# Attention with two MLPs: the mask's threshold computed on GpSimd in place of ScalarE

## The chip, the cores and the metric

The kernel runs on one core of a Trainium2 chip. A core has five engines with instruction queues of their own that are worked off in order: TensorE (PE; its weight loads are shown apart as PEld), VectorE (DVE), ScalarE (ACT), GpSimd (POOL) and SyncE (SP, which here only issues transfers). An instruction waits at the head of its queue until what it needs has been done on other engines, and everything behind it on that engine waits with it. The metric is the device time of one execution in microseconds (us).

## The reference

Attention over 4 batches, 8 heads, 576 positions and 64 features per head. A score counts only if it lies within tau of its row's maximum; the softmax is over what is left. The result goes through a gated MLP (512 to 1536 to 512) and a squared-ReLU MLP (512 to 2048 to 512).

```python
scores = scale * np.matmul(q, k.transpose(0, 1, 3, 2))
thresh = np.max(scores, axis=-1, keepdims=True) - tau
scores = np.where(scores >= thresh, scores, -1000000000.0)
scores = scores - np.max(scores, axis=-1, keepdims=True)
attn = np.exp(scores)
attn = attn / (np.sum(attn, axis=-1, keepdims=True) + 1e-09)
return np.matmul(attn, v).astype(np.float32)
...
x = _moe_ref(x=x, **moe_kwargs)      # silu(x @ w_gate) * (x @ w_val) @ w_out
return _moe2_ref(x=x, **moe2_kwargs) # relu(x @ w_in) ** 2 @ w_out
```

## The kernel before

There are two stages. The first, up to about 455 us, is attention in 144 tiles of 128 query rows by 576 keys (nine tiles for a pair of heads, 16 pairs). The second is the MLPs. While attention runs, matmuls of the gated MLP for batches that are done are put between its own on PE (`fill_group`, names `xs_m`, `m_th`, `m_u`, `w`), and weights are loaded and split into two parts of lower precision (`Loader`, names `wr`, `wf`, `w`).

Tile t goes through these steps, each a function of its own:

- `QK(t)`, L575, PE: scores into one of only two score buffers `s`, so QK(t+2) can't start before MASK(t) has read its buffer.
- `RED(t)`, L587, DVE: `nm`, the negative row maximum.
- `EXP(t)`, L593, ACT: exp(score - maximum) into `e`; and `thr` = maximum - tau, 128x1, one number per row, which is the instruction that changes (L595, or L598).
- `MASK(t)`, L604, DVE: sets e to zero where the score is under `thr`, and sums the row.
- `RCP(t)`, L610, DVE: `r`, the reciprocal of the sum. `NORM(t)`, L615, POOL: e times r.
- `TR(t)`, L635, PE, two tiles later: transposes of e. `PH` and `PL` (L655, L658, L665, L673, L56) take them out of PSUM in two parts `pt`, and `AV`, L694 (L691 for the first batch) multiplies by the values `vs`.

POOL has other work in its one queue: the low part of half of the weights (`w`, L56, which waits for a copy on ACT), the low part of k (`raw`, L56), the values' two parts (`vs`, L52 and L56), a small copy for the tail of each head (`qt`, L52), the low part of some `pt` (L56, from `tf`) and of the MLP's `m_u`. On ACT, `thr` stands beside exponentials and PSUM copies.

The program is written tile after tile, but a list scheduler then sets each engine's order by its own estimates of when each instruction can start, with the offsets in `early0` and `early` as priorities. So an edit of one instruction's engine changes the order of others as well, on every engine. The names below, such as `thr_5118`, carry a running number; `thr_240` is the threshold of tile 4 (tiles count from 0), `thr_267` of tile 5, `thr_1785` of tile 48, `thr_3094` of tile 75 and `thr_5118` of tile 120.

Of the kernel before, what the change touches and what calls it, by code (L numbers as in the profile page):

```python
# [18 lines left out]
P = 128  # L19
# [937 lines left out]
def pack(inputs):  # L957
# [48 lines left out]
    "u1": ("P", "P"),  # L1006
    "u2": ("A", "D"),
    "qs": "A",
    "thr": "A",
    "wl": "PD",  # L1010
    "live": (3, 2),
    "fill": 6,
# [35 lines left out]
```

## Time and profile before

| what | value |
|---|---|
| median of 3 runs (lowest, highest) | 1199.45 us (1198.36, 1200.13) |
| the profiled execution's own time | 1198.72 us |
| its span, first to last instruction | 1196.9 us |
| PE busy in the span | 1162.6 us (97%) |
| DVE, ACT, POOL busy | 868.2 (73%), 652.1 (54%), 293.8 us (25%) |
| L595, the threshold on ACT | 144 instructions, 42.3 us |
| first and last start of L595 | 12.3 and 451.8 us |

The busy shares are of the whole span. POOL does nothing after attention, so its 25% stands for a far fuller queue within the first 455 us. A busy PE is not PE at its peak, but time in which PE is not busy is lost for sure, since its work is the longest of all. "PEclk" is the granted clock of TensorE as a share of full speed.

### The profile page before, as it was taken

The numbers are of one execution on the slowest core, as the hardware profiler recorded it, in microseconds if no ns is written. First come the engines' busy times: TensorE is split into PE (matmuls) and PEld (weight loads), VectorE is DVE, ScalarE is ACT, GpSimd is POOL, SyncE is SP. The second block draws the span as 40 slices with busy tenths as digits, with TensorE's granted clock in tenths as the row PEclk, the third lists the DMA queues.
The fourth block names the chain that finished last, engine by engine and source line by source line (L and its number), as shares of the span: only waits on it lengthen the run. The fifth ranks groups of instructions, "written<-read, shape, count | busy, mean of one in ns | idle before, by whom it ended". The sixth has DMA issues, their size and how long they took to land.

```text
span 1196.9 us, 20191 instructions
## 1 busy us (share of the span) xinstructions
PE 1162.6 (97%) x7008; PEld 1074.8 (90%) x7008; DVE 868.2 (73%) x2143; ACT 652.1 (54%) x1622; POOL 293.8 (25%) x417
## 2 busy tenths in 40 slices
PE   5999998999999999999999999999999999999998
PEld 4555887999999999999999999999999899999997
DVE  6877997799989895789965954468449748754443
ACT  5777887888777774545432532145546425533221
POOL 4445875676776663000000000000000000000000
PEclk9999998999999999999999999999999999999999
DMA  5664452444334310332310300003002201100111
GB/s 177 151 182 127 127 134 66 109 116 110 94 97 106 93 36 1 108 104 80 98 36 7 108 29 1 1 18 104 21 1 80 62 1 54 36 1 1 53 54 53
DMA packets 40853, 84.79 MB, mean 71 GB/s; under 512 B 5936, under 2 KB 6960, under 8 KB 40752
## 3 DMA queue, kind: packets, MB, share of 16 engines
q1 hardware_dynamic: 40752, 83.52, 24.9%
q8 instruction: 55, 0.90, 0.3%
q14 instruction: 46, 0.38, 0.1%
HBM read 52.23 MB, written 4.72 MB: 48 GB/s over the span
## 4 chain that ended last, share of the span: by engine, by line
PE 79%; DVE 9%; DMA 3%; ACT 3%; issue 2%; POOL 2%; SPq 1%; POOLq 0%; DVEq 0%; ACTq 0%
PE mm L219 30%; PE mm L310 15%; PE mm L264 9%; PE s L575 5%; PE bank L635 5%; PE bank L219 4%; PE bank L264 4%; PE bank L694 4%; PE bank L691 3%; DMA wr<-in_w_dram 2%; DVE e L604 2%; DVE nm L587 1%; POOL e L615 1%; DMA raw<-in_qkv_dram 1%; DVE xs_k L56 1%
## 5 line engine op out<-in xcount | busy, mean ns | idle before, releaser
L219 PE MATMUL mm<-xs_k,w 128*128 128x384 f32 (+1 forms) x2400 | 413.2, 330 | 0.5 <-ACT x L48 0.5
L219 PEld LDWEIGHTS mm<-xs_k,w 128*128 128x128 f32 x2400 | 407.8, 188 | 2.5 <-ACT x L48 0.7
L310 PE MATMUL mm<-w,k_u 128*128 128x512 f32 x864 | 201.3, 391 | 0.3 <-DVE k_u L56 0.3
L310 PEld LDWEIGHTS mm<-w,k_u 128*128 128x128 f32 x864 | 161.5, 188 | 34.0 <-DVE k_u L56 1.0
L635 PE MATMUL bank<-ident,e 128*128 128x128 f32 x720 | 162.9, 278 | 6.4 <-POOL e L615 1.9
L219 PE MATMUL bank<-xs_m,w 128*128 128x288 f32 x720 | 137.1, 325 | 2.4 <-DVE xs_m L56 1.7
L615 POOL TENSOR_SCALAR e<-e,r 128x576 f32<-128x576 f32 x144 | 113.8, 791 | 83.6 <-DVE r L610 34.4
L604 DVE SCALAR_TENSOR_TENSOR e<-s,thr,e 128x577 f32<-128x577 f32 x144 | 117.0, 813 | 14.7 <-ACT thr L595 7.2
L48 ACT ACTIVATE k_u<-k_th 128x384 fp32r<-128x384 f32 (+1 forms) x148 | 76.3, 516 | 90.0 <-DVE k_th L294 47.0
L587 DVE TENSOR_REDUCE nm<-s 128x1 f32<-128x576 f32 x144 | 108.3, 753 | 17.7 <-PE s L575 16.6
L635 PEld LDWEIGHTS bank<-ident,e 128*128 128x128 f32 x720 | 95.2, 141 | 28.7 <-issue 15.9
L56 DVE TENSOR_TENSOR k_u<-k_th,k_u 128x384 fp32r<-128x384 f32 (+1 forms) x148 | 81.2, 549 | 47.8 <-ACT k_u L48 47.4
L219 PEld LDWEIGHTS bank<-xs_m,w 128*128 128x128 f32 x720 | 111.1, 189 | 5.1 <-DVE xs_m L56 3.4
L593 ACT ACTIVATE e<-s,nm 128x576 f32<-128x576 f32 x144 | 107.4, 746 | 14.3 <-PE bank L635 7.0
L655 ACT ACTIVATE pt<-bank 128x384 fp32r<-128x384 f32 (+1 forms) x216 | 92.1, 437 | 35.1 <-PE bank L635 28.9
L293 ACT ACTIVATE k_th<-mm 128x384 f32<-128x384 f32 x96 | 46.3, 483 | 111.0 <-PE mm L219 110.9
L264 PE MATMUL mm<-k_u,w 128*128 128x384 f32 (+1 forms) x624 | 106.1, 327 | 0.6 <-DVE k_u L56 0.4
L264 PEld LDWEIGHTS mm<-k_u,w 128*128 128x128 f32 x624 | 103.7, 188 | 1.0 <-DVE k_u L56 0.6
L694 PE MATMUL bank<-pt,vs 128*128 128x256 f32 (+1 forms) x480 | 93.5, 324 | 1.3 <-POOL pt L56 1.2
L575 PE MATMUL s<-kh,qs 128*128 128x288 f32 x256 | 78.1, 319 | 14.2 <-DVE qs L484 7.2
L294 DVE TENSOR_TENSOR k_th<-k_th 128x384 f32<-128x384 f32 x96 | 53.3, 555 | 52.4 <-ACT k_th L293 52.1
L48 ACT ACTIVATE w<-wf 128x256 fp32r<-128x256 f32 x116 | 46.8, 413 | 57.0 <-DVE wf L140 43.3
(90 smaller groups left out, 1697.0 us busy)
## 6 DMA issues: line engine op xcount, KB each, us to landing
wr<-in_w_dram SPq DMA_DIRECT2D x106, 256.0 KB, 3.0
raw<-in_qkv_dram SPq DMA_DIRECT2D x15, 896.0 KB, 4.7
kh<-land SPq DMA_DIRECT2D x60, 144.0 KB, 2.5
kl<-raw SPq DMA_DIRECT2D x60, 144.0 KB, 2.7
xF<-in_w_dram SPq DMA_DIRECT2D x30, 256.0 KB, 2.9
out_dram<-xF SPq DMA_DIRECT2D x18, 256.0 KB, 2.0
qs<-land SPq DMA_DIRECT2D x30, 144.0 KB, 2.4
qs<-raw SPq DMA_DIRECT2D x30, 144.0 KB, 2.6
```

What stands on the lines that cost most here:

```text
L48: nc.scalar.activation(out, in_, AF.Copy)
L56: e.tensor_tensor(out, a, b, op=ALU.subtract)
L219: mm(pt[:, :n], w[:, a, col + c * P : col + (c + 1) * P], xs[:, b, c, :], start=(i == 0), stop=(i == len(TERMS) - 1),)
L264: mm(pt[:, :n], w[:, a, 2 * DM + m * P : 2 * DM + (m + 1) * P], u[:, b, :], start=(k == 0), stop=(k == last),)
L310: mm(pt, u[:, b, s * P : (s + 1) * P], w[:, a, DM : 2 * DM], start=(k == 0), stop=(k == last),)
L575: mm(sp[:, cols], l, r[:, cols], start=(n_ == 0), stop=(n_ == len(pairs) - 1),)
L587: nc.vector.tensor_reduce(nm, sv, axis=AX.X, op=ALU.max, negate=True)
L593: nc.scalar.activation(e[:, :S], st[t]["s"][:, :S], AF.Exp, bias=st[t]["nm"])
L604: nc.vector.scalar_tensor_tensor(e, st[t]["s"][:, : S + 1], st[t]["thr"], e, op0=ALU.is_ge, op1=ALU.mult, accum_out=sum_)
L615: nc.gpsimd.tensor_scalar(e, e, scalar1=r, scalar2=1.0, op0=ALU.mult, op1=ALU.mult)
L635: mm(dst[:, j], e[:, c0 : c0 + P], ident, is_transpose=True, start=(j == 0), stop=(j == len(cols) - 1),)
L694: mm(o[:, :n], hd["vs"][:, SLOT[k % 5], :], pt[:, k, lo : lo + n], start=(k == 0), stop=(k == 9))
```

## The change

One entry of the configuration table is changed. `EXP` then takes its other branch, and `thr` comes from a GpSimd instruction that works out nm times -1 plus (-tau) for 128x1 elements, at L598 in place of the ScalarE one at L595.

```diff
     "qs": "A",
-    "thr": "A",
+    "thr": "P",
     "wl": "PD",
```

The scheduler then orders all five queues anew. Three places are shown, `+` for rows that stand there now, `-` for rows that stood there before. First POOL's queue at the start, around the thresholds of tiles 4 and 5 (`raw` is the low part of k, `qt` a small copy that waits for a transfer, `w_0` a weight's low part that waits for ACT).

```order
+L598 TENSOR_SCALAR thr_214<-nm_213,tau_n 128x1
+L56 TENSOR_TENSOR raw_205<-raw_205,land_207 128x288 x2
 L615 TENSOR_SCALAR e_97<-e_97,r_209 128x576
 L615 TENSOR_SCALAR e_95<-e_95,r_235 128x576
-L56 TENSOR_TENSOR raw_205<-raw_205,land_207 128x288 x2
 L52 TENSOR_SCALAR qt_122<-qs_333 128x64
+L56 TENSOR_TENSOR w_0_143<-xF,w_0_143 128x256
+L598 TENSOR_SCALAR thr_240<-nm_239,tau_n 128x1
+L598 TENSOR_SCALAR thr_267<-nm_266,tau_n 128x1
 L615 TENSOR_SCALAR e_96<-e_96,r_262 128x576
-L56 TENSOR_TENSOR w_0_143<-xF,w_0_143 128x256
```

The thresholds of tiles 4 and 5 stand behind six pieces of other work, and the weight's low part has moved ahead of them.

Second POOL's queue around the threshold of tile 120 (`vs` are the two parts of the next head's values).

```order
 L52 TENSOR_SCALAR vs_5379<-raw_5109 128x5x64
 L56 TENSOR_TENSOR vs_5379<-raw_5109,vs_5379 128x5x64
+L598 TENSOR_SCALAR thr_5118<-nm_5117,tau_n 128x1
 L615 TENSOR_SCALAR e_97<-e_97,r_5113 128x576
+L598 TENSOR_SCALAR thr_5163<-nm_5162,tau_n 128x1
 L615 TENSOR_SCALAR e_95<-e_95,r_5158 128x576
```

Nothing else moved there; the threshold stands behind both `vs` instructions and ahead of the NORM of the tile before.

Third PE's queue ahead of QK of tile 77 (the four rows of L575), which waits for MASK of tile 75; L219 are matmuls of the MLP, L694 those with the values.

```order
-L694 MATMUL bank_84<-pt,vs_2964 128x256
+L219 MATMUL bank_85<-xs_m_3173,w_0_143 128x288 x3
+L635 MATMUL bank_83<-ident,e_96 128x128 x2
+L219 MATMUL bank_85<-xs_m_3173,w_0_143 128x288
+L694 MATMUL bank_84<-pt,vs_2964 128x256 x3
+L219 MATMUL bank_85<-xs_m_3173,w_0_143 128x288 x2
+L694 MATMUL bank_84<-pt,vs_2964 128x256 x2
+L219 MATMUL bank_85<-xs_m_3173,w_0_143 128x288 x3
 L575 MATMUL s_108<-kh_3006,qs_3005 128x288
 L575 MATMUL s_108<-kl_3007,qs_3005 128x288
 L575 MATMUL s_108<-kh_3006,qs_3005 128x288
 L575 MATMUL s_108<-kl_3007,qs_3005 128x288
```

Here 16 matmuls stand ahead of QK that were not in this place before, in place of one there and two transposes a little earlier: 13 more than before. At QK of tile 122, which waits for MASK of tile 120, the number of matmuls ahead is the same as before.

## Rows read from the trace of the kernel before

**Rows 1.** Stages: us from:to, length, busy of each engine (instructions), PEclk, DMA share, GB/s.
```profile
30.00:120.00 90.00, 85.79 (x443) 52.44 (x442) 71.45 (x178) 66.16 (x172) 41.99 (x59) 1.00 0.57 153
120.00:200.00 80.00, 70.56 (x476) 64.31 (x475) 76.25 (x185) 66.11 (x178) 57.55 (x76) 0.96 0.42 114
200.00:455.00 255.00, 252.43 (x1915) 246.05 (x1914) 226.70 (x556) 200.78 (x513) 172.66 (x242) 1.00 0.38 92
```

**Rows 2.** PE's waits from 30 to 480 us: us in total, times, longest.
```profile
PE s L575 <- DVE e L604: 2.9, 4, 1.5
PE bank L264 <- POOL w L56: 1.8, 2, 1.6
...
PE bank L635 <- ACT pt L673: 1.7, 3, 1.0
PE bank L635 <- POOL e L615: 1.6, 3, 0.9
PE bank L694 <- POOL pt L56: 1.2, 3, 0.8
PE bank L635 <- ACT x L48: 0.9, 2, 0.7
PE bank L264 <- ACT w L48: 0.8, 1, 0.8
```

**Rows 3.** Threshold and mask by line: busy us, mean ns | idle before, releasers.
```profile
L604 DVE SCALAR_TENSOR_TENSOR e<-s,thr,e 128x577 f32<-128x577 f32 x144 | 117.0, 813 | 14.7 <-ACT thr L595 7.2 <-ACT e L593 5.0 <-PE bank L691 1.1
...
L595 ACT ACTIVATE thr<-nm,tau_n 128x1 f32<-128x1 f32 x144 | 42.3, 295 | 12.4 <-DVE nm L587 9.9 <-DVE r L610 1.6
```

**Rows 4.** POOL's smallest instructions, by tile and by line: ns least/median/most.
```profile
L52 POOL TENSOR_SCALAR qt<-qs x32: 235/246/433, 7.2 to 428.9; 128x64 fp32r<-128x64 f32 x32
...
L397 POOL MEMSET e<- x3: 99/99/100, 0.7 to 0.8; 128x1 f32 x3
```

**Rows 5.** Timeline of tile 4 (start, us; in brackets the idle time before, and its end).
```profile
21.82 0.81 DVE L604 SCALAR_TENSOR_TENSOR e<-s,thr,e 128x577 f32<-128x577 f32 x1
...
22.04 0.24 POOL L52 TENSOR_SCALAR qt<-qs 128x64 fp32r<-128x64 f32 x1
...
22.89 0.16 DVE L610 RECIPROCAL r<-sum 128x1 f32<-128x1 f32 x1
...
23.24 0.75 POOL L615 TENSOR_SCALAR e<-e,r 128x576 f32<-128x576 f32 x1 [0.96 <-DVE r L610]
...
23.55 0.40 PE L575 MATMUL s<-kh,qs 128*128 128x288 f32 x1
...
23.96 0.73 POOL L56 TENSOR_TENSOR w<-xF,w 128x256 fp32r<-128x256 f32 x1
```

**Rows 6.** Timeline of tile 120.
```profile
383.85 0.74 ACT L593 ACTIVATE e<-s,nm 128x576 f32<-128x576 f32 x1
...
384.80 0.82 DVE L604 SCALAR_TENSOR_TENSOR e<-s,thr,e 128x577 f32<-128x577 f32 x1
...
385.66 0.87 POOL L56 TENSOR_TENSOR vs<-raw,vs 128x320 fp32r<-128x320 f32 x1
...
386.79 0.29 PE L575 MATMUL s<-kh,qs 128*128 128x288 f32 x1
```

**Rows 7.** Timeline of tile 75.
```profile
249.42 0.82 DVE L604 SCALAR_TENSOR_TENSOR e<-s,thr,e 128x577 f32<-128x577 f32 x1 [0.32 <-ACT thr L595]
...
250.00 0.88 POOL L56 TENSOR_TENSOR vs<-raw,vs 128x320 fp32r<-128x320 f32 x1
...
250.30 0.40 PE L575 MATMUL s<-kh,qs 128*128 128x288 f32 x1
```

**Rows 8.** Timelines of POOL and DVE at tile 48.
```profile
153.13 0.74 POOL L56 TENSOR_TENSOR w<-xF,w 128x256 fp32r<-128x256 f32 x1 [1.52 <-ACT w L48]
...
154.53 1.74 POOL L56 TENSOR_TENSOR raw<-raw,land 128x288 fp32r<-128x288 f32 x2
...
152.88 0.81 DVE L604 SCALAR_TENSOR_TENSOR e<-s,thr,e 128x577 f32<-128x577 f32 x1
```

## The prediction

> **What bounds the kernel now.** I read the busy time by stage first. From 200 to 455 us PE is busy 252.43 of 255 us, so it sets the end of attention there; from 120 to 200 us it is busy 70.56 of 80, with DVE at 76.25 as the fuller engine and a mean granted clock of 0.96; from 30 to 120 us PE lacks 4.2 us of 90 [rows 1]. All three together leave 16.2 us in which PE stands idle, and since the change touches no instruction after attention, a gain can come from little else. Whether it comes depends on who ends those waits. In the list of PE's waits the three kinds that ACT ends make 1.7 + 0.9 + 0.8 = 3.4 us in 6 waits, the three longest kinds that POOL ends 1.8 + 1.6 + 1.2 = 4.6 us in 8, and MASK ends 2.9 us in 4 [rows 2]. So ACT, which the change relieves, holds PE up for less time than POOL, which it loads.
>
> Then the threshold itself. MASK sat idle 7.2 us for `thr` and 5.0 us for the exponential [rows 3]. The first number looks like the gain, and the reader should see why it is not. ACT sends `thr` off right behind the exponential: at tile 120 the exponential ends at 383.85 + 0.74 = 384.59 and MASK starts at 384.80, with the threshold between [rows 6]. Without it MASK still waits for the exponential, and wins some 0.2 us. And in front of none of PE's four waits for MASK had that MASK started right behind its threshold: DVE was at other work until then. I book 0.2 us, one such MASK in the first 30 us, which the list leaves out.
>
> **What the change removes, adds and moves.** Removed: 144 ACT instructions of 295 ns, 42.3 us [rows 3]. ACT is not full in any stage, 66 of 80 us at its fullest [rows 1], so this is worth what PE's waits for ACT shrink by: one threshold of 0.295 us in front of each of the 6 waits gives 1.8 us, none gives 0, all of the waits gone gives 3.4. I take 1.8, since an average of one threshold stands between two such copies.
>
> Added: 144 POOL instructions of 128x1. The trace has none of them. From below, a memset of 128x1 takes 99 ns; from above, a TENSOR_SCALAR of 128x64, the same operation with 63 more columns, 246 ns in the median and 433 at most [rows 4]. A NORM of 576 columns takes 0.75 us, so 512 columns more than 64 cost 0.50, one column 1 ns; that leaves 0.19 us for one column, which I take. Hand-offs: NORM starts 23.24 where its reciprocal ended 23.05, 0.19 later [rows 5]; the way out to DVE has no row here, it lies between 0 and that, and I take 0.05, since the 0.21 us between exponential and MASK at tile 120 already hold most of a threshold of 0.295. A threshold on a free POOL then reaches MASK 0.43 us after RED's end, while the exponential, which waits for the same RED, takes 0.74 [rows 6]. So on a free queue the threshold is wholly hidden. The price is in the queue.
>
> That price has two parts. The smaller: POOL's own work that PE waits for gets later by the thresholds in front of it. 8 waits, 0.19 each, would be 1.5 us; not every run of POOL work that ends in such a wait has a threshold in it, so I take half, 0.8 (bounds 0 and 1.5).
>
> The larger: the head of POOL's queue. `thr` now waits until the instruction ahead of it is done, and MASK waits for `thr`, with DVE's whole queue behind it and QK two tiles later on PE. I went through the new POOL order, took for each threshold the end of the instruction ahead of it in the trace of before, added 0.19 + 0.05, and compared it with the start of its MASK; then subtracted the time by which QK of two tiles later started after that MASK's end. Two tiles show the working. Tile 120: `vs` ends 385.66 + 0.87 = 386.53, so MASK could start at 386.77 in place of 384.80, 2.0 late; its old end was 385.62 and QK came at 386.79, 1.1 us of slack, so 0.85 reaches PE [rows 6]. Its neighbours on POOL and on PE are as before, so nothing covers that. Tile 75: `vs` ends at 250.88, MASK would be 1.7 late, and QK started within 0.06 us of its end [rows 7], so all of 1.7 reaches PE by this account. But there the scheduler has put 13 more matmuls ahead of that QK; at the stage's rate of 255 us for 1915 matmuls, 0.13 each [rows 1], they fill 1.7 us. This one is covered.
>
> Over all tiles ten keep something past the slack, from tile 4 (2.2) to tile 120 (0.85), 10.9 us in sum. Then I take off what the order itself answers. Tiles 75 and 77, 2.1: covered by matmuls that moved. Tiles 4 and 5, 3.4: the account uses `w` at its old time of 23.96, but `w` has moved up; right behind `qt`, which ended 22.28, it would end 23.0, MASK start 23.25 in place of 21.82, 1.4 late against a slack of 0.9 [rows 5], so I keep 1.0 of the 3.4. Tile 48, 2.0: the low part of k ahead of its threshold ran after two `w` that took from 153.13 to 154.53, and these now stand behind it [rows 8]; MASK was at 152.88, so between 0.6 and 2.0 stays, and I keep 1.0. That leaves 10.9 - 2.1 - 2.4 - 1.0 = 5.4.
>
> A page of the Trainium skill speaks against this engine too: GPSIMD Engine Reference, section Key points, says that GpSimd shares its SBUF interfaces with VectorE and that they contend when a DVE instruction has two SBUF inputs. The 128x64 copy took between 235 and 433 ns [rows 4], which agrees with some such disturbance without showing its cause. By that rule every late threshold could cost 0.43 in place of 0.19, 2.4 us over ten tiles. I leave this out of the sum.
>
> **Sum.** 5.4 (late masks) + 0.8 (POOL's other work) - 1.8 (ACT) - 0.2 (the threshold's own wait) = +4.2 us. The profiled execution took 1198.72, 0.7 under the median of 1199.45; the same 4.2 on the median gives 1203.7.
>
> **Rivals.** First, faster: ACT's relief wins. Late masks cost nothing because the scheduler moved work under each as it did at tile 75, and all six waits for ACT go: -3.4 - 0.2 gives 1195.8. For it speaks that ACT's exponentials and copies share one queue; against it that tile 120 has no cover. It decides if fewer than about 1.2 us of late masks reach PE while the 3.4 us go whole, since then 2.4 us (0.2%, about what a measurement of this kernel tells from no change) are won.
>
> Second, no difference that can be told: masks are late, but half of the 5.4 is absorbed because a PE that waits once finds its next inputs ready. Then 2.7 + 0.8 - 1.8 - 0.2 = +1.5, 1201.0. For it speaks that the waits of DVE and of PE are counted here tile by tile, as though none made up for another; against it that PE from 200 us on is full and has nothing to make up with.
>
> Third, slower by more than 9 us: neither moved matmuls nor moved POOL work cover anything, and each threshold hits the waits in POOL's queue: 10.9 + 1.5 - 0 = +12.4, 1211.9. The stage from 120 to 200 us, where DVE is nearly full and the clock already sags, is where it would show. Against it stand the moves read at tiles 75, 4 and 48.
>
> That the change does nothing at all is excluded by the new order.
>
> **How the numbers follow.** The forecast case, slower by 2.4 to 9 us, gets 0.46; slower by more 0.07; no difference 0.26; faster 0.21. So faster 0.21, same 0.26, slower 0.53. The range: from 1196.5, which leaves the lower half of the faster case out, to 1209.5, under the third rival; about 1 in 10 is left on each side. The forecast case by itself reaches from 1201.9 to 1208.5.
>
> **What would show it.** In the profile after, L598 on POOL should show about 0.19 us each, 27 us in all, and L595 be gone from ACT. MASK (L604) should show idle time that POOL's `thr` ended, more than the 7.2 us of before, in waits of 1 to 2 us behind `vs`, `raw` and `w`; at tile 120 PE should wait for MASK some 0.8 us ahead of QK of tile 122. PE's busy time from 200 to 455 us should stay, and its idle time in the attention stage grow by 4 us. I am wrong if MASK waits less for POOL than it did for ACT, if a threshold takes 0.1 us or 0.4, or if the idle time from 120 to 200 us shrinks because the order there happens to fit better, which this account can't see.

## The result and the profile after

The changed kernel takes 1209.14 us in the median (1208.33 to 1210.54 in 6 runs), the kernel before 1199.05 beside it; the ratio of the means is 1.0081, with an interval of 1.0066 to 1.0095. That is 9.7 us slower (0.81% of 1199.45), with 1.7 to either side; the medians lie 10.1 apart. The forecast was slower by 4.2, 1203.7, in a range from 1196.5 to 1209.5. The sign and the range hold. The size does not: 9.7 is more than twice 4.2, and just outside the forecast case's own range, which ended at 1208.5.

The profiled execution took 1208.33 us, with a span of 1206.6. Busy time by engine, first on its page:

```profile
PE 1166.8 (97%) x7008; PEld 1076.0 (89%) x7008; DVE 867.9 (72%) x2143; ACT 628.1 (52%) x1478; POOL 333.4 (28%) x561
```

PE's busy time grew by 4.2 us from 1162.6, for the same 7008 matmuls, and its idle time in the span by 5.5, from 34.3 to 39.8. The profile models the ends of matmuls, so a short delay can also lie inside what it counts as busy. ACT lost 24.0 us of 652.1 and POOL's busy time grew by 39.6. The 144 instructions on ACT summed to 42.3 us [rows 3], but they overlapped the exponential ahead of them (at tile 120 it ends at 384.59, and MASK, which needs the threshold of 0.295 too, starts 0.21 later [rows 6]); so only 24.0 us of busy time went.

The same lines as in [rows 3], and the new one (busy us, mean ns, then idle time of the engine ahead of them and what ended it):

```profile
L598 POOL TENSOR_SCALAR thr<-nm,tau_n 128x1 f32<-128x1 f32 x144 | 44.8, 312 | 52.3 <-DVE nm L587 31.3 <-DVE r L610 18.6 <-PE s L575 2.1
...
L604 DVE SCALAR_TENSOR_TENSOR e<-s,thr,e 128x577 f32<-128x577 f32 x144 | 117.2, 815 | 29.3 <-ACT e L593 13.5 <-POOL thr L598 9.7 <-POOL e L615 1.6
```

MASK's idle time doubled, from 14.7 to 29.3 us. The threshold now ends 9.7 of it where it ended 7.2; but the exponential ends 13.5 where it ended 5.0. So the larger part of the growth isn't put down to the threshold, which is the first sign that MASK's new wait isn't the whole story.

The stages of [rows 1] (us from:to, length, busy time of PE, PEld, DVE, ACT, POOL, granted clock, DMA):

```profile
30.00:120.00 90.00, 84.62 (x429) 51.01 (x430) 67.80 (x173) 60.41 (x139) 49.19 (x89) 1.00 0.54 140
120.00:200.00 80.00, 70.47 (x471) 62.90 (x469) 76.79 (x185) 60.97 (x152) 65.89 (x97) 0.97 0.50 136
200.00:455.00 255.00, 248.96 (x1859) 240.26 (x1859) 222.23 (x543) 181.79 (x419) 188.97 (x318) 1.00 0.37 91
```

PE's idle time in them is 5.4 + 9.5 + 6.0 = 20.9 us, where it was 16.2. The growth of 4.7 is nearly all from 200 us on (3.5) and from 30 to 120 us (1.2). It is about half of the 9.7.

PE's waits of [rows 2], from 30 to 480 us (total, times, longest):

```profile
PE s L575 <- DVE e L604: 3.9, 10, 0.7
PE bank L665 <- ACT pt L655: 3.0, 3, 1.5
PE bank L635 <- POOL e L615: 2.9, 3, 1.6
PE bank L264 <- POOL w L56: 1.8, 3, 0.8
...
PE bank L635 <- ACT x L48: 1.0, 2, 0.5
...
PE bank L264 <- ACT w L48: 0.8, 2, 0.4
```

MASK ends ten of them where it ended four. And the three longest kinds that ACT ends make 4.8 us where they made 3.4: the engine that was relieved holds PE up for longer. The list of before has a fourth kind that ACT ends, which [rows 2] leaves out; with all kinds ACT's are 4.1 us before and 5.9 after.

```profile
PE bank L665 <- ACT pt L655: 0.7, 2, 0.4
```

Tile 120, in three stretches of the timeline after (start, us, engine; in brackets the idle time before it and what ended it):

```profile
394.99 0.87 POOL L56 TENSOR_TENSOR vs<-raw,vs 128x320 fp32r<-128x320 f32 x1
395.85 0.27 POOL L598 TENSOR_SCALAR thr<-nm,tau_n 128x1 f32<-128x1 f32 x1
...
396.15 0.82 DVE L604 SCALAR_TENSOR_TENSOR e<-s,thr,e 128x577 f32<-128x577 f32 x1 [1.07 <-POOL thr L598]
...
397.03 0.40 PE L575 MATMUL s<-kh,qs 128*128 128x288 f32 x1 [0.52 <-DVE e L604]
```

It went as forecast for this tile in kind: the threshold stands behind `vs`, MASK waits 1.07 us for it with DVE idle, and PE waits for MASK ahead of QK of tile 122, for 0.52 us where 0.85 had been worked out.

### The profile page after: what moved, and what is told of

Same layout as the page of the kernel before. It is cut to its first block, busy times and chain, and to the rows that moved or that the text cites. A ratio compares the mean times of both kernels' runs of the same rounds, so it can differ in the third digit from the quotient of the medians.

```text
span 1206.6 us, 20253 instructions
## 1 busy us (share of the span) xinstructions
PE 1166.8 (97%) x7008; PEld 1076.0 (89%) x7008; DVE 867.9 (72%) x2143; ACT 628.1 (52%) x1478; POOL 333.4 (28%) x561
## 4 chain that ended last, share of the span: by engine, by line
PE 82%; DVE 7%; POOL 6%; issue 3%; ACT 2%; DMA 0%; SPq 0%; POOLq 0%; ACTq 0%; DVEq 0%
PE mm L219 34%; PE mm L310 16%; PE mm L264 9%; PE bank L219 5%; PE s L575 4%; PE bank L635 4%; PE bank L694 3%; PE bank L264 3%; PE bank L691 3%; DVE e L604 2%; POOL e L615 1%; DVE nm L587 1%; POOL pt L56 1%; POOL raw L56 1%; DVE xs_m L56 1%
## 5 line engine op out<-in xcount | busy, mean ns | idle before, releaser
L219 PE MATMUL mm<-xs_k,w 128*128 128x384 f32 (+1 forms) x2400 | 413.2, 330 | 0.5 <-ACT x L48 0.5
L219 PEld LDWEIGHTS mm<-xs_k,w 128*128 128x128 f32 x2400 | 407.8, 188 | 2.5 <-ACT x L48 0.7
L635 PE MATMUL bank<-ident,e 128*128 128x128 f32 x720 | 162.1, 279 | 8.8 <-POOL e L615 4.9
L219 PE MATMUL bank<-xs_m,w 128*128 128x288 f32 x720 | 137.2, 325 | 2.4 <-DVE xs_m L56 1.3
L604 DVE SCALAR_TENSOR_TENSOR e<-s,thr,e 128x577 f32<-128x577 f32 x144 | 117.2, 815 | 29.3 <-ACT e L593 13.5
L635 PEld LDWEIGHTS bank<-ident,e 128*128 128x128 f32 x720 | 95.1, 142 | 30.1 <-issue 13.2
L615 POOL TENSOR_SCALAR e<-e,r 128x576 f32<-128x576 f32 x144 | 110.3, 766 | 31.2 <-DVE r L610 15.2
L219 PEld LDWEIGHTS bank<-xs_m,w 128*128 128x128 f32 x720 | 111.1, 189 | 6.1 <-DVE xs_m L56 2.5
L56 DVE TENSOR_TENSOR k_u<-k_th,k_u 128x384 fp32r<-128x384 f32 (+1 forms) x148 | 81.1, 549 | 46.2 <-ACT k_u L48 45.8
L575 PE MATMUL s<-kh,qs 128*128 128x288 f32 x256 | 78.8, 322 | 15.9 <-DVE e L604 7.6
L694 PE MATMUL bank<-pt,vs 128*128 128x256 f32 (+1 forms) x480 | 92.6, 323 | 1.4 <-DVE xF L706 0.8
L694 PEld LDWEIGHTS bank<-pt,vs 128*128 128x128 f32 x480 | 74.7, 193 | 3.1 <-DVE xF L706 1.0
```

The costliest lines, as they stand in the source:

```text
L56: e.tensor_tensor(out, a, b, op=ALU.subtract)
L219: mm(pt[:, :n], w[:, a, col + c * P : col + (c + 1) * P], xs[:, b, c, :], start=(i == 0), stop=(i == len(TERMS) - 1),)
L575: mm(sp[:, cols], l, r[:, cols], start=(n_ == 0), stop=(n_ == len(pairs) - 1),)
L604: nc.vector.scalar_tensor_tensor(e, st[t]["s"][:, : S + 1], st[t]["thr"], e, op0=ALU.is_ge, op1=ALU.mult, accum_out=sum_)
L615: nc.gpsimd.tensor_scalar(e, e, scalar1=r, scalar2=1.0, op0=ALU.mult, op1=ALU.mult)
L635: mm(dst[:, j], e[:, c0 : c0 + P], ident, is_transpose=True, start=(j == 0), stop=(j == len(cols) - 1),)
```

## Where the time is lost along the kernel

To follow the loss I took the start of the first matmul (L575) of QK of eight tiles in each trace, and subtracted its start in the trace of before. The experiments' kernels are told below. Each column is one execution, so a stretch at TensorE's lower clock level, which comes at other places in other executions, shifts it too. e5 has one at 107.5 to 110.3 us (7 matmuls), between tiles 30 and 62. From 180 to 205 us the granted clock is 0.86 in before, after, e5 and e12, 0.93 in e7 and e8, and 1.00 in e10; from 205 to 455 us it is 1.00 in all of them, so the steps behind tile 62 are free of it. e5's execution was also the slowest of its six, 1209.67 us where their median is 1205.44, so its column stands too high; it has another low stretch behind attention (granted clock 0.76 from 515 to 522 us).

| QK of tile | start before, us | after | e5 | e7 | e8 | e10 | e12 |
|---|---|---|---|---|---|---|---|
| 5 | 19.41 | 0.4 | 1.0 | 0.1 | 1.7 | 0.6 | 0.4 |
| 6 | 23.55 | 2.3 | 2.9 | 0.1 | 3.2 | 0.7 | 3.8 |
| 30 | 88.94 | 3.3 | 4.0 | 0.2 | 4.2 | 0.7 | 3.8 |
| 62 | 208.05 | 6.2 | 8.0 | 0.0 | 6.1 | -0.1 | 3.7 |
| 76 | 248.60 | 6.2 | 7.9 | 0.0 | 6.1 | 0.0 | 3.7 |
| 88 | 282.76 | 8.8 | 8.8 | 2.7 | 6.2 | 0.5 | 3.7 |
| 123 | 391.07 | 10.4 | 8.8 | 4.4 | 6.3 | 0.7 | 3.7 |
| 143 | 450.31 | 11.1 | 9.0 | 5.1 | 6.3 | 1.0 | 3.8 |
| (end of the span) | 1196.9 | 9.7 | 11.0 | 4.5 | 5.6 | 0.8 | 4.1 |

In the changed kernel 2.3 us are lost by tile 6, some 4 more by tile 62, nothing between 62 and 76, and 4.9 in steps behind tile 76, of which 1.4 come back behind attention. The forecast's late masks sit in those last steps; the 6.2 us ahead of them lie where it had booked 2.7, and e5 will show that they come without late masks too.

## The experiments

Three theories stood against one another. **Head of the queue**, the forecast's: MASK waits for a threshold that stands behind other POOL work. **Load**: 40 us more work on POOL makes its other products late. **Order**: the scheduler's new order fits worse, whoever computes the threshold. Each ratio is to runs of the kernel before on the same chip, and is turned into microseconds of 1199.5. e1, e5 and e6 leave out the comparison with the tile's own threshold, so they tell of the time alone.

**e1: the changed kernel, MASK not waiting for POOL.** Order, load and ACT's relief stay.

```diff
-            e, st[t]["s"][:, : S + 1], st[t]["thr"], e, op0=ALU.is_ge, op1=ALU.mult, accum_out=sum_
+            e, st[t]["s"][:, : S + 1], st[t]["nm"], e, op0=ALU.is_ge, op1=ALU.mult, accum_out=sum_
```

> The changed kernel with the threshold still worked out on GpSimd in all 144 tiles, in exactly the same order on every engine, but MASK compares the scores with nm in place of thr (so the threshold is computed and not used). Only MASK's wait for GpSimd is gone; the load on GpSimd, the relief of ScalarE and the new order stay. Head of the queue (MASK waits for a threshold that stands behind other GpSimd work): nearly all of the loss goes, 1199 to 1202.5 us. Load (144 more instructions make GpSimd's other work late): 1207 to 1209. Reorder (the new order fits worse, whoever computes the threshold): 1207 to 1209. By the terms of the prediction: 1209.1 less the late masks, so the before kernel plus 0.8 for load less 1.8 for ScalarE, about 1198.

Measured: 1204.91 us, ratio 1.0047 (1.0031 to 1.0062), 5.6 us over before. It fell between the theories. Some 4 us of the 9.7 went with the wait (4.1, with 2.5 to either side), and more than half stayed, though MASK no longer waits for anything of POOL's:

```profile
L604 DVE SCALAR_TENSOR_TENSOR e<-s,nm,e 128x577 f32<-128x577 f32 x144 | 116.9, 814 | 18.1 <-ACT e L593 16.7
```

**e5: the same with other numbers.** In e1 the numbers in the matmuls differ from the changed kernel's, since nearly all scores pass its mask. So the wait was taken away once more in a way that keeps most of them out.

```diff
-            e, st[t]["s"][:, : S + 1], st[t]["thr"], e, op0=ALU.is_ge, op1=ALU.mult, accum_out=sum_
+            e, st[t]["s"][:, : S + 1], st[max(t - 1, 0)]["thr"], e, op0=ALU.is_ge, op1=ALU.mult, accum_out=sum_
```

> The changed kernel in exactly its own order on every engine, but MASK compares with the threshold of the tile before its own, which GpSimd has finished long before; so the wait is gone as in e1, and about as few scores pass the mask as in the changed kernel (in e1 nearly all pass, so that the numbers in the matmuls differ). If e1's 5 us above the kernel before come from the order: again 1203.5 to 1206. If they came from its numbers (a lower clock): 1199 to 1202. If MASK's wait were all of the loss: 1199 to 1200.5.

Measured: 1205.44 us, ratio 1.0050 (1.0036 to 1.0064), 6.0 us over before. So the numbers aren't it: with the wait gone and the order kept, some 6 us stay. Tile 120 shows the wait gone in full. MASK starts ahead of the threshold of its own tile, with no idle time before it, and QK behind it with none:

```profile
394.39 0.82 DVE L604 SCALAR_TENSOR_TENSOR e<-s,thr,e 128x577 f32<-128x577 f32 x1
...
395.13 0.27 POOL L598 TENSOR_SCALAR thr<-nm,tau_n 128x1 f32<-128x1 f32 x1
...
395.62 0.30 PE L575 MATMUL s<-kh,qs 128*128 128x288 f32 x1
```

In the table e5 loses 0.9 us from tile 76 to 123 where the changed kernel loses 4.2. PE's waits in the same trace, that of the slow execution, show what ends those that remain:

```profile
PE bank L635 <- POOL e L615: 4.0, 4, 1.6
PE bank L665 <- ACT pt L655: 3.5, 3, 1.5
PE bank L264 <- ACT w L48: 2.6, 4, 1.3
...
PE bank L635 <- ACT x L48: 1.0, 2, 0.5
```

Those three kinds that ACT ends make 7.1 us here (4.7 in e1), against 3.4 in [rows 2], on an ACT with 144 instructions less.

**e2: the load by itself.** The kernel before, in its own order, with one more POOL instruction of 128x1 behind each NORM.

```diff
         nc.gpsimd.tensor_scalar(e, e, scalar1=r, scalar2=1.0, op0=ALU.mult, op1=ALU.mult)
+        twin = sm.tile([P, 1], F32, name=f"twin{t}", tag="twin")
+        nc.gpsimd.tensor_scalar(twin, r, scalar1=-1.0, scalar2=tau_n, op0=ALU.mult, op1=ALU.add)
```

> The kernel before, with its threshold on ScalarE and exactly its order on every engine, and one more GpSimd instruction per tile behind NORM: 128x1, the same operation as the threshold, read by nobody (work is added, none is left out). Load alone. Head of the queue: within 1 us of the kernel before, 1198.5 to 1200.5. Load: most of the loss appears, 1204 to 1209. Reorder: as before, 1199. In all three the new instruction should take 0.25 to 0.3 us, 36 to 44 us in all.

Measured: 1198.98 us, ratio 1.0000 (0.9989 to 1.0010). The load costs nothing that can be told, though it is all there:

```profile
L617 POOL TENSOR_SCALAR twin<-r,tau_n 128x1 f32<-128x1 f32 x144 | 44.4, 308 | 0.0
```

Load falls as a theory, for the order of before.

**e3 and e4: ten tiles, both ways.** The ten tiles of the forecast's account, put back on ACT in the changed kernel (e3), or put on POOL alone in the kernel before (e4). Of e3, and of e4, the branch in `EXP`:

```diff
-        if cfg["thr"] == "A":
+        if t in (4, 5, 44, 48, 75, 77, 80, 85, 93, 120):
```

```diff
-        if cfg["thr"] == "A":
+        if t not in (4, 5, 44, 48, 75, 77, 80, 85, 93, 120):
```

> The changed kernel with the threshold of ten tiles (4, 5, 44, 48, 75, 77, 80, 85, 93, 120), those of the prediction's late masks, back on ScalarE; 134 stay on GpSimd, and the order is that of the changed kernel but for some 40 of 11,000 instructions. Head of the queue, with the ten tiles as its seats: the steps at tiles 80, 85, 93 and 120 (4.0 us together) go and some of the start, 1203 to 1206. Head of the queue, but spread over all the tiles that start right behind their threshold: 1206 to 1208. Load or reorder: 1208 to 1210.

> The kernel before with the threshold of the same ten tiles (4, 5, 44, 48, 75, 77, 80, 85, 93, 120) on GpSimd; 134 stay on ScalarE, and the order is that of the kernel before but for some 85 of 11,000 instructions. Head of the queue: these ten alone bring a good part of the loss, 1202 to 1206. Load: 10 of 144 instructions, under 1 us, 1199 to 1200. Reorder: almost no reorder here, 1198.5 to 1200.

Measured: e3 1206.59 us, ratio 1.0059 (1.0044 to 1.0073); e4 1199.08 us, ratio 0.9997 (0.9988 to 1.0006). e3 wins back 2.6 of the 9.7, and MASK's idle time for POOL's threshold falls from 9.7 to 4.2 us, so the ten tiles hold over half of that wait. e4 is a miss for the head of the queue: the same ten tiles cost nothing in the other order. Its trace says in part why. At tile 120 the threshold stands ahead of `vs` in that order, not behind it:

```profile
386.17 0.27 POOL L598 TENSOR_SCALAR thr<-nm,tau_n 128x1 f32<-128x1 f32 x1
386.40 0.46 POOL L52 TENSOR_SCALAR vs<-raw 128x320 fp32r<-128x320 f32 x1
386.94 0.87 POOL L56 TENSOR_TENSOR vs<-raw,vs 128x320 fp32r<-128x320 f32 x1
```

Tiles 80, 85 and 93 are late there: QK of tile 95 starts 2.3 us later against before than QK of tile 76 (+1.1 and -1.2). But that trace had won 1.3 us by tile 62. From 180 to 205 us its granted clock is 0.93 where before has 0.86, one stretch at the lower level less, which can be what it won; whether each execution wins it isn't shown. So a late mask's price can be read from the place, but the sum over a kernel can't.

**e6: no threshold at all.** Relief of ACT, and no load for POOL. Its edit is to the kernel before; the tiles of the threshold are left out too, and a constant is added.

```diff
-    tau_n = cpool.tile([P, 1], F32, name="tau_n")
+    tau_n, thc = (cpool.tile([P, 1], F32, name=n) for n in ("tau_n", "thc")); nc.vector.memset(thc, 0.011)
...
-        th = sm.tile([P, 1], F32, name=f"thr{t}", tag="thr")
+        th = None
...
-            nc.scalar.activation(st[t]["thr"], st[t]["nm"], AF.Identity, scale=-1.0, bias=tau_n)
...
-            e, st[t]["s"][:, : S + 1], st[t]["thr"], e, op0=ALU.is_ge, op1=ALU.mult, accum_out=sum_
+            e, st[t]["s"][:, : S + 1], thc, e, op0=ALU.is_ge, op1=ALU.mult, accum_out=sum_
```

> No threshold at all on any engine: MASK compares with a constant of 0.011 (near the usual threshold, one more memset at the start), so the 144 threshold instructions are left out. The order comes out near that of the changed kernel (all but 141 of its 6928 PE rows and 79 on ScalarE and GpSimd stand alike) and unlike the kernel before (640 PE rows). Order: 1203 to 1206, as e1, though less work is done than in either kernel. Load on GpSimd in this order: 1199 to 1201. By the relief of ScalarE, as the prediction booked it, 1197 to 1198.5.

Measured: 1211.02 us, ratio 1.0089 (1.0075 to 1.0103). With 144 instructions left out it is 10.7 us slower, as slow as the changed kernel, with no threshold to wait for. But not all of that is the order of attention. QK of tile 143 starts 8.0 us late in its trace, near e1's 9.4 and e5's 9.0, and the end of the span comes 12.6 late. The rest lies in the matmuls of the MLP stage, which take longer each there at a granted clock of 1.00 and with hardly a wait; first two lines of e6, then the same of the changed kernel:

```profile
L219 PE MATMUL mm<-xs_k,w 128*128 128x384 f32 (+1 forms) x2400 | 416.2, 332 | 0.5 <-ACT x L48 0.5
L310 PE MATMUL mm<-w,k_u 128*128 128x512 f32 x864 | 203.2, 393 | 0.0
...
L219 PE MATMUL mm<-xs_k,w 128*128 128x384 f32 (+1 forms) x2400 | 413.2, 330 | 0.5 <-ACT x L48 0.5
L310 PE MATMUL mm<-w,k_u 128*128 128x512 f32 x864 | 200.9, 390 | 0.0
```

That is 5.3 us, which none of the other traces has, and no run shows its cause. If e6's other runs have it too, it leaves 5.4 of the 10.7 as an estimate, which is what e1 and e5 have. So order, which e6 shares with the changed kernel, costs that much with no threshold on any engine. e6 also tells where the new order comes from. In the first tiles POOL's queue has `raw` ahead of the NORMs of tiles 2 and 3, as in the changed kernel:

```profile
19.60 1.90 POOL L56 TENSOR_TENSOR raw<-raw,land 128x288 fp32r<-128x288 f32 x2 [2.83 <-ACT land L48]
21.48 1.47 POOL L615 TENSOR_SCALAR e<-e,r 128x576 f32<-128x576 f32 x2
```

There is no instruction on POOL here that wasn't there before. So that piece of the order follows from the threshold's absence on ACT, not from its presence on POOL.

**e7 and e8: by place.** The threshold on POOL from tile 57 on alone, or up to tile 56 alone, again in `EXP`:

```diff
-        if cfg["thr"] == "A":
+        if t < 57:
```

```diff
-        if cfg["thr"] == "A":
+        if t >= 57:
```

> The threshold on GpSimd in tiles 57 to 143 alone, in 0 to 56 on ScalarE; the order up to there is that of the kernel before, and in all 112 of 6928 PE rows differ. MASK's wait (the changed kernel gathers 4.8 us from tile 57 on, e1 only 0.6): 1202 to 1205. Order: the few moved rows bring little, 1199 to 1201. As e4, where ten tiles cost nothing by the times: 1199 to 1200.

> The threshold on GpSimd in tiles 0 to 56 alone, in 57 to 143 on ScalarE; up to there the order is that of the changed kernel (131 of 6928 PE rows differ from it). Order: 5 to 6.5 us over the kernel before, 1204 to 1206.5, as e1. MASK's wait alone, which sits mostly behind tile 57: 1199 to 1202.

Measured: e7 1205.14 us, ratio 1.0041 (1.0027 to 1.0055), 4.9 us; e8 1204.26 us, ratio 1.0035 (1.0023 to 1.0047), 4.2 us. Together 9.1 of the 9.7. In the table e7 runs with the kernel before to within 0.3 us up to tile 76 and then climbs in steps to 5.1; e8 has its whole loss by tile 62 and is flat behind it. So there are two losses in two places. MASK's line in e7, and tile 120, which repeats that of the changed kernel:

```profile
L604 DVE SCALAR_TENSOR_TENSOR e<-s,thr,e 128x577 f32<-128x577 f32 x144 | 117.1, 814 | 25.3 <-POOL thr L598 9.3 <-ACT thr L595 6.8 <-ACT e L593 4.4
...
390.13 0.82 DVE L604 SCALAR_TENSOR_TENSOR e<-s,thr,e 128x577 f32<-128x577 f32 x1 [1.07 <-POOL thr L598]
```

**e10: e7 with the held masks let go.**

```diff
-        if t < 57:
+        if t < 57 or t in (59, 74, 75, 77, 80, 85, 93, 94, 102, 116, 120, 133, 135):
```

> e7 (threshold on GpSimd from tile 57 on) less the thirteen tiles whose MASK in e7 started within 0.12 us of its threshold and over 0.25 us behind its exponential (59, 74, 75, 77, 80, 85, 93, 94, 102, 116, 120, 133, 135), which are back on ScalarE; 74 stay on GpSimd. 54 of 6928 PE rows differ from e7. MASK's wait: all of e7's 5 us go, 1199 to 1201. Order or load: 1203 to 1206, as e7. If 74 thresholds less on ScalarE bring anything: under 1198.5.

Measured: 1200.04 us, ratio 1.0006 (0.9991 to 1.0020), 0.7 us. Thirteen thresholds back on ACT take away 4.2 of e7's 4.9 us. With e1 and e5 this shows the wait: 3.7 to 4.2 us by three comparisons, each with some 2.5 us to either side. MASK's line shows what is left:

```profile
L604 DVE SCALAR_TENSOR_TENSOR e<-s,thr,e 128x577 f32<-128x577 f32 x144 | 117.1, 814 | 17.8 <-ACT thr L595 6.3 <-ACT e L593 4.3 <-POOL thr L598 1.6
```

It also prices the relief of ACT where little stands against it: 74 thresholds gone from ACT, 1.6 us of MASK's idle time ended by those on POOL, and no gain that can be told (the interval reaches from 1.1 us faster to 2.4 slower).

**e12 and e9: the start.** e12 has the threshold on POOL in tiles 0 to 8 alone; e9 is the changed kernel with `raw` behind the two NORMs again.

```diff
-        if cfg["thr"] == "A":
+        if t >= 9:
```

```diff
-        off = cfg["early0" if fstate["i"] < 9 * NPAIR else "early"].get(name or f.__name__, 0)
+        off = cfg["early0" if fstate["i"] < 9 * NPAIR else "early"].get(name or f.__name__, 0); off = 8 if name == "PS" and fstate["i"] < 6 else off
```

> The threshold on GpSimd in tiles 0 to 8 alone, in 9 to 143 on ScalarE; in those first tiles the order is that of the changed kernel, behind them that of the kernel before (20 of 6928 PE rows differ from it). If the first part of the loss (e8: 4 us for tiles 0 to 56) arises in the first 30 us, as the traces have it (2.3 to 3 us by tile 6): 1201.5 to 1203. If it arises between tiles 9 and 56: 1199 to 1200.5.

> The changed kernel with the threshold of all tiles on GpSimd, and one piece of its order put back as it was before: in the first tiles the low part of k (raw, two instructions that wait for a copy on ScalarE) stands behind the NORMs of tiles 2 and 3 again. PE, VectorE and SyncE keep the changed kernel's order, 2 rows move on ScalarE and 4 on GpSimd. If the first part of the loss is that raw ahead of NORM: 2 to 3 us under the changed kernel, 1206 to 1207.5. If it is the thresholds of tiles 4 and 5 behind w, as the prediction had it (they stay behind it): 1208.5 to 1210.

Measured: e12 1201.78 us, ratio 1.0022 (1.0010 to 1.0034), 2.6 us; e9 1209.25 us, ratio 1.0076 (1.0053 to 1.0100). e12 puts more than half of e8's loss into the first nine tiles. (Its trace has 3.8 us by tile 6, more than the times, with 7 matmuls at the lower clock level between 23.8 and 26.6 us.) POOL and PE there, in e12:

```profile
19.25 1.90 POOL L56 TENSOR_TENSOR raw<-raw,land 128x288 fp32r<-128x288 f32 x2 [1.31 <-ACT land L48]
21.14 1.46 POOL L615 TENSOR_SCALAR e<-e,r 128x576 f32<-128x576 f32 x2
...
21.93 0.44 PE L635 MATMUL bank<-ident,e 128*128 128x128 f32 x2 [1.48 <-POOL e L615]
```

In the kernel before, the two NORMs ran from 19.02 and `raw` behind them from 20.52. Here `raw` waits 1.31 us for ACT at the head of the queue, and PE then waits 1.48 us for the NORM behind it. The same wait of 1.47 to 1.48 us stands in the traces of the changed kernel, e1, e3, e5 and e6. That looked like the cause, and e9 should have won it back. Its times show no gain, though their interval, 6.4 to 12.0 us over before, would leave room for one of 2 us. Its trace can't settle it: the wait is gone, but PE worked at the lower clock level up to 23.0 us (last section) and was 2.9 us late at tile 6 all the same. In e8, which has `raw` ahead and a low stretch as long, that wait doesn't show either.

**e11: the threshold on VectorE.**

```diff
-    "thr": "P",
+    "thr": "D",
```

> The threshold on VectorE in all 144 tiles, so that MASK finds it on its own engine and waits for no other but the exponential; order unlike both (1078 PE rows differ from the kernel before, 680 from the changed one). A reciprocal of 128x1 takes 0.155 us there, so 22 us more work for VectorE, some 25 of them, 4 us, in the stage from 120 to 200 us where it has 4 us free. MASK's wait for GpSimd as the only cause: 1199 to 1203. Order as the greater cause: 1204 to 1210.

Measured: 1213.33 us, ratio 1.0111 (1.0085 to 1.0138), 13.3 us. The instruction takes 0.207 us there, 29.4 in all, and MASK waits for no engine but ACT. By the head of the queue alone it should have been near before. This doesn't part order from DVE's own new work, which is 29 us.

No version tried beats the kernel before.

## Why the prediction was right, and where it wasn't

**What bounds the kernel** was read rightly in the main. PE's idle time from 30 to 455 us grew by 4.7 us, where the forecast had said 4; but that is half of the loss, and the other half isn't waits that the profile shows. PE's busy time from 200 to 455 us, which was to stay, fell from 252.43 to 248.96. MASK's idle time for the threshold grew from 7.2 to 9.7, and tile 120 went step by step as written, at about half the size.

**Late masks, +5.4 booked.** The mechanism is shown, by e1, e5 and by e10 against e7, at 3.7 to 4.2 us. The single places are off both ways. Behind tile 76, where 2.7 were booked (tiles 80, 85, 93 and 120), e7 loses 5.1 and e10 1.0, so 4.1 are the masks'; e10's list shows tiles 94, 133 and 135 among those held too, which the account had let pass. Before tile 57, where 2.7 were booked (tiles 4, 5, 44 and 48), no run shows any: e5, which has no such wait, loses no less by its times (6.0 us, of which its trace puts 1.0 behind tile 76) than e8, in which those thresholds are on POOL and MASK waits for them, and which loses 4.2. Tiles 75 and 77 were taken off as covered, and rightly: in e7 QK of tile 80, behind both of the QKs that they would hold up, is level with before (0.1 us ahead).

**The threshold's price, 0.19 booked**, is 0.265 in the median and 0.312 in the mean, 44.8 us in all instead of 27. The median is even above the bound from above, the 128x64 copy at 0.246 [rows 4]: 63 columns less saved nothing. The extrapolation of one nanosecond per column from a long instruction down to a short one failed. The spread up to 1.2 us has a place in the trace. 36 of the 144 thresholds ran beside one of six lines on DVE whose wide operands all lie in SBUF (L527, L132, L134, L138, L140, and `xs_m` at L56), and took 0.265 to 1.202 us, 0.356 in the median; the other 108 took 0.255 to 0.273. The longest of all:

```profile
427.40 1.20 POOL L598 TENSOR_SCALAR thr<-nm,tau_n 128x1 f32<-128x1 f32 x1 [1.27 <-DVE nm L587]
...
427.75 0.80 DVE L527 SCALAR_TENSOR_TENSOR raw<-raw,qscale,land 128x576 fp32r<-128x576 f32 x1
```

The rule of the Trainium skill on shared SBUF interfaces (GPSIMD Engine Reference, Key points) was weighed at 0.43 for every late threshold. The trace agrees with the rule where DVE had two SBUF inputs, as at L527, with up to 1.2 us; at tile 120 the threshold took 0.27.

**POOL's other work, +0.8 booked**, is 0.0 by e2, with 1.3 us to either side, so 0.8 isn't excluded.

**The threshold's own wait, -0.2**, is too small for any run here to show.

**ACT's relief, -1.8 booked**, is the step that failed: "one threshold of 0.295 us in front of each of the 6 waits gives 1.8 us". It priced the relief in the old order (and by 3.4 us in 6 waits, where the list in full has 4.1 in 8). Once the thresholds were off ACT the scheduler ordered much of the rest anew: by the two traces 270 of ACT's 1478 instructions and 351 of PE's 7008 matmuls stand elsewhere in their queues (buffer numbers left aside). In the new order PE's waits for ACT grew, from 3.4 to 4.8 us in the three longest kinds. The words "what the order itself answers" took the reorder as cover alone, something to take off. It is a cost of its own, 5.6 to 6.0 us by e1 and e5 with the relief in it, and e6 has a cost of that kind with no threshold on any engine. PE's waits for ACT are a small part of it.

So the sum of the forecast is +4.2 and the parts measured are about 4 for the wait, 0 for the load, and 5.6 to 6.0 for order and relief together. The wait was mis-sized by a little; the order was missing. The late masks alone would have put the kernel on the right side and near the forecast's 4.2. That the whole loss, more than half of it from a cost that the forecast didn't know, still ended inside the range, 0.4 us under its upper end, is luck.

**The rivals.** Faster, by ACT's relief, is refuted by the result, and e10, where 74 thresholds are off ACT, shows no gain. No difference is refuted by the result. Slower by more than 9 us is where the time fell, but not by its mechanism, in which nothing covers a late mask: tiles 75 and 77 were covered.

**What stays open.** Of the order's cost, 2.6 us lie in the first nine tiles (e12), and the last section shows that the clock isn't needed for them; e9 leaves it unsettled how much `raw` ahead of NORM makes and how much PE's own new order there. For the other 3 or so one place shows in every trace. Take the time from the start of each transpose (L635) to the start of the next matmul, less the idle time that the profile counts: its sum is 50.6 us in before and 54.0 in the changed kernel, 53.5 to 54.5 in e1, e3, e5, e6, e8 and e9, which have its order of the early tiles or nearly so, and 50.9 to 51.8 in e2, e4, e7, e10 and e12, which don't (e12 has it up to tile 8). What stretches the transposes isn't shown. Part can be the clock: the granted clock, as the mean over the runs, is 0.9963 for the changed kernel, 0.9962 to 0.9967 for e1, e3, e5, e6 and e8, and 0.9979 to 0.9984 for the runs of before beside the experiments. As an estimate that is some 2 us (0.0018 of 1206) if PE's pace is the limit throughout; no run parts it from the order. Why e4's ten tiles cost nothing in sum isn't settled either.

## What to carry to other kernels

In a kernel that a list scheduler orders, an instruction that moves to another engine is two changes: the move, and a new order on every engine. Price them apart, by running the new order with the new wait taken away and the old order with the new load put in; here the wait cost about 4 us, the order about 6, and the load, in the old order, nothing that could be told. And ask of a small instruction what stands ahead of it in its new queue, not how full that engine is: thirteen of e7's 87 thresholds carried nearly its whole price, and to leave those where they were cost one line.

## What the runs showed of the hardware

The same 128x1 operation takes 0.295 us on ACT, 0.265 in the median on POOL and 0.207 on DVE; on POOL 64 columns take no longer, 0.246 [rows 4]. On POOL it took up to 1.2 us beside DVE instructions on wide SBUF operands, and never more than 0.273 in the changed kernel otherwise.

How long PE works at its lower clock level at the start differs from one execution to another. After its wait for the first MASK it begins there in every trace. In the kernel before the last matmuls at that pace start at 16.0 us, in the changed one at 17.2, and in three traces (e2, e8, e9) at 22.6 to 23.0; e2 has the order of before. First of the kernel before, then of e9, matmuls of the same shape:

```profile
13.90 0.44 PE L575 MATMUL s<-kl,qs 128*128 128x288 f32 x1
14.14 0.44 PE L575 MATMUL s<-kh,qs 128*128 128x288 f32 x1
...
19.75 0.29 PE L575 MATMUL s<-kh,qs 128*128 128x288 f32 x1
19.89 0.29 PE L575 MATMUL s<-kl,qs 128*128 128x288 f32 x1
```

```profile
21.24 0.44 PE L575 MATMUL s<-kl,qs 128*128 128x288 f32 x1
21.48 0.44 PE L575 MATMUL s<-kh,qs 128*128 128x288 f32 x1
21.72 0.44 PE L575 MATMUL s<-kl,qs 128*128 128x288 f32 x1
```

One starts every 0.24 us in the first pair, 288 columns at 1.2 GHz, and every 0.14 in the second, near 2.4 GHz; e9 is still at the first pace at 21.72. The granted clock of the page shows 1.00 in all of these stretches, so the pace has to be read from the matmuls. e2, whose order is that of before, is 2.6 us late at tile 6 in its trace, as much as the changed kernel loses there. So up to tile 6 a single trace can't tell an order's cost from the clock's. Traces whose first low stretch ended alike can: the last matmuls at the low pace start at 17.2 to 17.8 us in the changed kernel, e1 and e5, which are 2.3 to 2.9 us late at tile 6, and at 17.3 to 17.8 in e4, e7 and e10, which start in or near the order of before and are 0.1 to 0.7 late. About 2 us there are the order's.
